# A new order of all steps for a linear-attention and squared-ReLU kernel, with stores on GpSimd and five more transposes by DMA

## The chip, the cores and the metric

The kernel runs on one core of one Trainium2 chip. A core has four compute engines that run their own instruction queues in order, and one that only issues transfers: TensorE (PE in the profile; PEld is its weight load, which overlaps the matmuls), VectorE (DVE), ScalarE (ACT), GpSimd (POOL) and SyncE (SP). Transfers between DRAM and the on-chip memory SBUF are issued by an engine's queue and carried out by 16 DMA engines. TensorE writes to PSUM, which this kernel uses as eight banks of 128 x 512 float32. The metric is the device time of the kernel in microseconds; the median of three runs before the change is 175.57 us (175.53 to 176.38).

## What is computed

```python
for t in range(S):                                       # linear attention, per batch b and head h
    cur = u * k[t] outer v[t]
    y[t] = r[t] @ (state + cur)
    state = w * state + k[t] outer v[t]                  # w decays each of the 48 rows of the state
x = y.transpose(0, 2, 1, 3).reshape(3072, 384)           # 4 x 768 tokens, 8 heads of 48
h = maximum(x @ w_in, 0)                                 # w_in 384 x 2048
out = (h * h) @ w_out                                    # w_out 2048 x 384
```

Batch 4, 8 heads, 768 steps, head size 48; all inputs and the output are float32. The kernel multiplies in bfloat16.

## The kernel before

**Tiles.** The 768 steps of a batch are cut into six chunks of 128. A unit is one chunk of one batch with all eight heads; there are 24, and unit i is chunk i // 4 of batch i % 4. Within a unit the recurrence is written as matrix products; from chunk to chunk a batch hands on a small state, S0W. The feed-forward layer then takes units in groups: units 0 and 1 by themselves (groups 0 and 1), the other 22 in pairs (groups 2 to 12).

**Steps of a unit.** Each step is a small function of the class `Do`, and its name is what the order and this text use:

- `ld.r.i`, `ld.k.i`, `ld.v.i` (L320) load 192 KB each, in rows of 192 bytes. `P0` (L342) multiplies r and k, `P1` (L346) multiplies that by u, `du` (L349) sums over the head, `dv` (L354) multiplies v by the sum.
- `kh` (L336) and `rh` (L339) scale k and r by powers of the decay and write bfloat16; for the first four units they take the powers from PSUM, later from SBUF. `vb` (L260, L262) casts v.
- The scaled r and k are transposed, either by `T` (L363, eight transposes on TensorE) and the copy `Tc` to SBUF, or by `XB` (L369), one transposing DMA of SP.
- `A` (L376), eight small matmuls; `Bm` (L384) masks the result, once for each half; `Y` (L392, L394) multiplies by v and, from the second chunk on, by the state; `xs` (L411) adds dv.
- `U` (L403) makes the state's increment; `S0` (L418), or `ts` (L421) and `S` (L424), write the new state.
- x is transposed by `X` (L429, three transposes on TensorE) and the copy `xTc`, or by `xX` (L436), one transposing DMA of SP.

**Steps of a group.** `F1.g.s` (L445) makes one PSUM bank of x @ w_in, 12 matmuls of 128 columns for a single unit, 6 of 256 for a pair; `re` (L453 on ACT, L455 on DVE) takes the maximum with zero, `sq` (L460 ACT, L462 or L464 DVE) squares. `F2.i.q` (L472) adds four matmuls of 384 columns for unit i, q = 0 to 3; `os` (L260, L262) copies the 128 x 384 result to SBUF and `out` (L489) stores it.

**Weights.** Seven of the eight pieces of w_in come as float32 by `lW.0.s` (L324, 384 KB, four buffers) and are cast by `cW.0.s`; piece 2 comes by `W.0.2` and w_out by `W.1.0` to `W.1.3` (L333), DMAs of GpSimd that cast on their way. For a pair `F1.g.s` needs piece s; for a single unit F1.g.0 needs pieces 0 and 1, F1.g.1 pieces 2 and 3, and so on. `w`, `u` and `wc` load the decay and u, `Wk`, `Wt`, `WkS`, `WtS`, `WLcol` and `WLm` make the tables from them. `Z.n.b` is n filler matmuls of no use to the result, which occupy TensorE at the start.

**What sets the order.** Nothing is planned at run time. The string ORDER lists 963 steps, each as step:engine/buffers, for example `re.1.3:D/2`: A is ACT, D is DVE, G is GpSimd, P is TensorE, S is SP, and the numbers say which buffer each new tile gets from its pool (L19; 7 buffers for each of r, k and v, 30 for hq, 2 PSUM banks each for F1 and F2). The loop at L498 issues the steps as they stand. Each engine thus has a fixed queue, and an instruction that must wait for its input or for its buffer holds back all behind it on its engine. Waits are added where one step reads what another writes.

Of the kernel before, what the change touches and what calls it, by code (L numbers as in the profile page):

```python
# [20 lines left out]
ld.r.1:S/0 w:A ld.k.1:S/0 u:S Z.48.5:P tab:A ld.k.0:S/1 ld.k.2:S/2 shw:D ld.r.0:S/1 logw:A ld.r.2:S/2 Wt:A/0 P0.1:D/0  # L21
shu:D Wk:A/1 lW.0.6:S/0 rh.1:D/0 kh.1:D ld.v.1:S/0 ld.k.3:S/3 T.1:P/0 kh.0:D/1 Z.16.5:P P1.1:G Tc.1:A/0 kh.2:D/2 rh.0:D
ld.v.3:S/1 WtS:A rh.2:D P0.2:G/1 A.1:P/1/2 WkS:A T.0:P/3 lW.0.1:S/1 Z.16.5:P P1.2:D ld.r.3:S/3 Tc.0:A/1 du.1:D/0
P0.0:D/2 cW.0.6:A ld.v.0:S/2 A.0:P/0/3 dv.1:G Bm.1.1:D/0 Z.6.5:P du.2:D/1 T.2:P/2 P1.0:G Bm.1.0:D/1 ld.v.2:S/3 Z.22.5:P
Tc.2:A/2 Bm.0.0:D/2 Bm.0.1:D/3 lW.0.0:S/2 vb.1:A/0 lW.0.5:S/3 kh.3:D/3 Y.1:P/1 cW.0.1:A lW.0.7:S/0 A.2:P/0/2 xs.1:D/0
Z.4.5:P P0.3:G/3 vb.3:A/1 du.0:D/2 lW.0.4:S/1 X.1:P/3 Z.8.5:P rh.3:D wc:S xTc.1:A/0 Bm.2.0:D/4 vb.0:A/2 T.3:P/1
ld.k.4:S/4 dv.0:D Y.0:P/3 Z.13.5:P Tc.3:A/3 vb.2:G/3 Bm.2.1:D/5 P1.3:G xs.0:D/1 A.3:P/0/2 X.0:P/1 cW.0.0:A U.0:P/3
dv.2:G Bm.3.0:D/1 Z.6.7:P xTc.0:A/1 du.3:D/3 lW.0.3:S/2 F1.1.0:P/0 Bm.3.1:D/0 ld.r.4:S/4 F1.0.0:P/1 re.1.0:D/0 W.1.0:G
W.0.2:G cW.0.7:G Y.2:P/0 Y.3:P/1 re.0.0:A/1 ld.k.5:S/5 xs.2:D/2 cW.0.5:A dv.3:D F1.1.3:P/0 cW.0.4:A X.2:P/2 F1.0.3:P/1
re.1.3:D/2 ld.r.5:S/5 xTc.2:A/0 W.1.1:G U.2:P/0 xs.3:D/3 F1.0.2:P/0 re.0.3:A/3 sq.1.3:D2/0 WLcol:A X.3:P/2 F1.1.2:P/1  # L30
re.0.2:D/4 xTc.3:A WLm:G U.3:P/1 F1.2.1:P/0 re.1.2:A/5 W.1.2:G sq.0.3:A0/1 F1.2.5:P/1 re.2.1:D/2 W.1.3:G sq.0.0:A0/2
U.1:P/2 S0.2:D re.2.5:A/3 F1.2.4:P/0 sq.0.2:D2/3 cW.0.3:A S0.0:D F1.2.7:P/1 re.2.4:D/1 sq.1.0:A0/4 F2.0.0:P/1
# [12 lines left out]
ld.k.12:S/5 sq.3.3:A0/18 Y.7:P/2 out.3:S kh.10:D/3 re.3.6:A/4 Y.6:P/1 ld.v.8:S/3 S.4:G xs.7:D/1 F1.3.2:P/0 sq.3.5:A0/19
xs.6:D/2 F1.3.7:P/1 ld.v.11:S/1 kh.8:D/0 re.3.2:A/0 kh.15:D/4 U.6:P/0 X.6:P/3 sq.3.2:A0/20 X.7:P/2 rh.8:D F2.4.0:P/1
ld.r.12:S/4 re.3.7:A/5 rh.10:D F2.5.1:P xTc.6:A/2 sq.3.4:D2/21 P1.9:D xTc.7:A U.7:P/1 T.8:P/3 vb.9:A/2 out.0:S P0.8:D/4
F1.4.0:P/0 ts.6:D/1 ld.k.11:S/0 Tc.8:A/2 P1.8:G ts.7:D/0 F1.4.4:P/1 ld.r.13:S/5 du.9:D/3 re.4.0:A/2 F2.5.2:P kh.12:G/5
re.4.4:A/3 F1.4.6:P/0 ld.r.11:S/0 sq.3.6:A0/23 sq.3.7:D2/22 vb.8:G/3 du.8:D/4 A.9:P/2/0 sq.4.4:A0/24 A.8:P/1/3 S.6:G
re.4.6:A/0 F2.5.3:P ld.v.10:S/5 Bm.8.1:D/4 F1.4.3:P/1 dv.8:G Bm.8.0:D/5 os.5:A/3 ld.k.13:S/6 F1.4.5:P/0 Bm.9.1:D/1  # L50
re.4.3:A/1 dv.9:G Y.8:P/3 Bm.9.0:D/0 re.4.5:A/5 XB.10:S/3 F2.4.1:P P0.12:G/0 xs.8:D/3 sq.4.0:A0/25 Y.9:P/1 vb.11:A/1
# [57 lines left out]
    A=["bA{0}0", "bA{0}1"],  # L109
    ld=["{0}{1}"],  # L110
    lW=["ws{0}{1}"], kh=["rk{0}"], rh=["rk{0}"], P0=["P{0}"], du=["dv{0}"], vb=["vb{0}"], T=["bT{0}"], Tc=["rkT{0}"], XB=["rkT{0}"],
    Bm=["Bm{0}{1}"], Y=["bY{0}"], xs=["xs{0}"], U=["bU{0}"], ts=["ts{0}"], X=["bX{0}"], re=["hr{0},{1}"], sq=["hq{0},{1}"],
    F1=["bH{0},{1}"], os=["os{0}"], Wk=["WkP"], Wt=["WtP"],
)


@with_exitstack
def kernel(
# [13 lines left out]
    B, H, S, D = r.shape  # L132
# [409 lines left out]
```

## Time and profile before

| quantity | value |
|---|---|
| median of the runs | 175.57 us |
| profiled execution's span, first to last instruction | 174.6 us (the median is 0.97 us longer) |
| granted TensorE clock, mean | 0.998 |
| busy: PE, DVE, ACT, POOL | 164.3, 140.6, 109.4, 69.4 us |
| filler matmuls Z within PE | 11.1 us (139 matmuls) |
| last matmul ends | 171.1 us |
| DMA: moved in all, on the queue of SP | 28.36 MB, 26.20 MB |

How it is to be read: busy time is the time in which an engine has an instruction in work. The page gives it for the whole span and in 40 slices; a table of stretches gives it for any window. An engine that is busy without a break for a long stretch sets the pace there. The table of groups gives the mean duration of each kind of instruction and the idle time ahead of it with what ended it. A timeline lists single instructions with their start, duration and, in brackets, the idle time before them. For a DMA the engine's row shows the issue only; the landing is seen in the page's table of DMA issues (median us from issue to landing) or in an instruction that waited for it.

### The profile page before, as it was taken

To read this page: it belongs to the slowest core of one execution; us is meant where nothing else is said; L and a number is where in the kernel's file an instruction comes from. 1 tells how busy PE (TensorE), PEld (TensorE's weight loads), DVE (VectorE), ACT (ScalarE), POOL (GpSimd) and SP (SyncE) were. 2 spreads that over 40 slices of the span, in tenths; PEclk is the share of its full clock that TensorE was granted. 3 is DMA by queue.
4 is the path that set the end of the run, shared out by engine and by line. 5 is a ranking of instruction groups with operands and counts; after the bars stand their busy time and mean duration, and the time that the engine had idled before them with its cause. 6 is when DMAs were issued, how large, how long until landed. Compare 5 with 4: busy or idle time off the path is not lost.

```text
span 174.6 us, 4605 instructions
## 1 busy us (share of the span) xinstructions
PE 164.3 (94%) x1813; PEld 127.1 (73%) x1813; DVE 140.6 (80%) x279; ACT 109.4 (63%) x203; POOL 69.4 (40%) x85
## 2 busy tenths in 40 slices
PE   3978599999999999999999999999999999999991
PEld 3967488866778777877767787777778677787760
DVE  5779677799899989999989898899988667853620
ACT  3578479549499987786677669669478142164410
POOL 5253834044366594925373960700950302000000
PEclk9999999999999999999999999999999999999999
DMA  4989999989799999999998989989931422110041
GB/s 99 228 194 240 320 200 237 207 155 213 144 205 177 231 217 165 233 157 252 152 214 187 195 164 220 160 196 230 164 94 26 158 90 71 24 45 4 0 165 61
DMA packets 102421, 28.36 MB, mean 162 GB/s; under 512 B 94840, under 2 KB 102400, under 8 KB 102400
## 3 DMA queue, kind: packets, MB, share of 16 engines
q1 hardware_dynamic: 100504, 26.20, 72.6%
q0 software_dynamic: 1744, 1.77, 6.3%
q8 instruction: 14, 0.23, 0.5%
q10 hardware_dynamic: 152, 0.10, 0.2%
q14 instruction: 7, 0.06, 0.1%
HBM read 20.46 MB, written 4.72 MB: 144 GB/s over the span
## 4 chain that ended last, share of the span: by engine, by line
PE 84%; DMA 6%; SPq 4%; POOL 1%; issue 1%; ACT 0%; DVE 0%; POOLq 0%
PE bank L472 36%; PE bank L445 36%; DMA wsa<-in_moe_w_in_dram 6%; SPq L320 4%; PE bank L376 3%; PE bank L394 2%; PE bank L392 2%; PE bank L403 2%; PE bank L363 2%; PE bank L429 1%; POOL W L262 1%; SPq L324 0%; POOL urow L218 0%; ACT vb L260 0%; DVE os L262 0%
## 5 line engine op out<-in xcount | busy, mean ns | idle before, releaser
L445 PE MATMUL bank<-xT,W 128*128 128x256 bf16 (+1 forms) x624 | 74.4, 264 | 2.3 <-ACT W L260 2.1
L472 PE MATMUL bank<-W,hq 128*128 128x384 bf16 x384 | 73.6, 326 | 0.0
L453 ACT ACTIVATE hr<-bank 128x512 bf16<-128x512 f32 x71 | 42.0, 597 | 36.8 <-PE bank L445 34.2
L445 PEld LDWEIGHTS <-W 128*128 128x128 bf16 x624 | 55.4, 98 | 12.6 <-ACT W L260 2.2
L472 PEld LDWEIGHTS <-hq 128*128 128x128 bf16 x384 | 35.6, 98 | 17.8
L460 ACT ACTIVATE hq<-hr 128x512 bf16<-128x512 bf16 x57 | 34.7, 629 | 2.5 <-DVE hr L455 2.2
L384 DVE TENSOR_TENSOR Bm<-bank,maskJT 128x512 bf16<-128x512 f32 x48 | 31.4, 682 | 3.1 <-PE bank L376 3.0
L346 POOL TENSOR_TENSOR P<-P,ub 128x384 f32<-128x384 f32 x14 | 15.2, 1087 | 30.2 <-DVE P L342 27.4
L354 POOL TENSOR_TENSOR dv<-ldv,du 128x384 f32<-128x384 f32 x19 | 16.4, 874 | 25.0 <-DVE du L349 21.0
L455 DVE TENSOR_SCALAR hr<-bank 128x512 bf16<-128x512 f32 x25 | 17.1, 688 | 11.2 <-PE bank L445 7.5
L464 DVE TENSOR_TENSOR hq<-hr 128x512 bf16<-128x512 bf16 x35 | 15.0, 456 | 1.7 <-ACT hr L453 1.7
L411 DVE TENSOR_TENSOR xs<-bank,dv 128x384 bf16<-128x384 f32 x24 | 13.2, 553 | 3.2 <-PE bank L394 2.5
L481 PE MATMUL bank<-identity 128*128 128x128 bf16 x139 | 11.1, 244 | 2.7 <-POOL identity masks.py:199 2.7
L260 ACT COPY os<-bank 128x384 f32<-128x384 f32 (+1 forms) x18 | 8.4, 469 | 8.1 <-PE bank L472 8.1
L342 POOL TENSOR_TENSOR P<-ldr,ldk 128x384 f32<-128x384 f32 x11 | 11.3, 1025 | 4.8 <-DMA ldr<-in_r_dram 4.8
L349 DVE TENSOR_REDUCE du<-P 128x8 f32<-128x384 f32 x24 | 12.9, 542 | 0.0
L260 ACT COPY rkT<-bank 128x1024 bf16<-128x1024 bf16 x10 | 10.1, 1016 | 3.4 <-PE bank L363 3.3
L481 PEld LDWEIGHTS <-identity 128*128 128x128 bf16 x139 | 9.8, 112 | 2.9 <-POOL identity masks.py:199 2.7
L424 POOL TENSOR_TENSOR S0W<-ts,WLm 128x384 bf16<-128x384 f32 x7 | 7.4, 1061 | 10.0 <-PE bank L472 6.7
L394 PE MATMUL bank<-vb,Bm 128*128 128x48 bf16 x192 | 10.8, 183 | 0.5 <-ACT vb L260 0.5
L394 PEld LDWEIGHTS <-Bm 128*128 128x128 bf16 x192 | 9.5, 96 | 1.5 <-issue 0.8
L260 ACT COPY xT<-bank 128x384 bf16<-128x384 bf16 x14 | 6.5, 478 | 5.1 <-PE bank L429 5.1
(62 smaller groups left out, 167.1 us busy)
## 6 DMA issues: line engine op xcount, KB each, us to landing
ldr<-in_r_dram SPq DMA_DIRECT2D x24, 192.0 KB, 3.8
ldk<-in_k_dram SPq DMA_DIRECT2D x24, 192.0 KB, 3.9
ldv<-in_v_dram SPq DMA_DIRECT2D x24, 192.0 KB, 3.6
out_dram<-os SPq DMA_DIRECT2D x23, 192.0 KB, 2.1
wsa<-in_moe_w_in_dram SPq DMA_DIRECT2D x7, 384.0 KB, 5.9
W<-in_moe_w_out_dram POOLq DMA_DIRECT2D x4, 384.0 KB, 7.6
rkT<-rk SPq DMA_TRANSPOSE x14, 4.2
W<-in_moe_w_in_dram POOLq DMA_DIRECT2D x1, 192.0 KB, 8.8
```

The costliest lines, as they stand in the source:

```text
L260: e.copy(o, a)
L346: e.tensor_mul(t, t, ub)
L354: e.tensor_mul(dvb[slot[f"dv{i}"]], loaded("v", i), t)
L384: e.tensor_mul(Bmb[slot[f"Bm{i}{h}"]], heads(bank(f"bA{i}{h}"), 128), mask_b)
L394: e.matmul(y[:, hc, D * h : D * (h + 1)], m[h][:, hc, :], vb[:, 2 * hc + h, :], start=(c == 0), stop=True, skip_group_check=True,)
L445: e.matmul(hp[:, fi, :], W1[f // 2][:, c, 128 * (f % 2) : 128 * (f % 2 + 1)], xt[:, c, :], start=(c == 0), stop=(c == CCH - 1), skip_group ...
L453: e.activation(hr, hp, AF.Relu)
L455: e.tensor_scalar_max(hr, hp, 0.0)
L460: e.activation(hq, hr, AF.Square)
L464: e.tensor_mul(hq, hr, hr)
L472: e.matmul(bank(f"bO{i}", "bO")[:, 0:d_model], hqb[slot[f"hq{g},{f // m}"]][:, at : at + L], W2[q][:, f % 4, :], start=(f == 0), stop=(f = ...
L481: e.matmul(banks[b][:, 0:128], identity, identity, start=True, stop=True, skip_group_check=True)
```

## The change

All steps are put in a new order, and many change their engine or buffer; 956 are left. The F2 steps go from 96 to 92, and two steps of a new kind, F2c, are added. Pools, buffers and the functions of the other steps are the same.

- Loads stay on SP in another order: the first eight are k.2, r.0, u, r.2, r.1, k.0, v.0, r.3, and the two small DMAs of `wc`, which stood behind the weight loads, now come tenth.
- Fifteen of the 24 stores of SP are issued by GpSimd instead; nine stay on SP, and half of the last tile on ACT, where it was.
- Units 7, 8 and 11 are transposed by `XB` instead of `T` and `Tc` (7 T, 17 XB), units 13 and 19 by `xX` instead of `X` and `xTc` (12 X, 12 xX).
- Element-wise work moves between engines, mostly to GpSimd:

| step | before | after |
|---|---|---|
| P0 | 13 DVE, 11 POOL | 7 DVE, 17 POOL |
| P1 | 10 DVE, 14 POOL | 8 DVE, 16 POOL |
| kh | 19 DVE, 5 POOL | 9 DVE, 15 POOL |
| rh | 18 DVE, 6 POOL | 13 DVE, 11 POOL |
| vb | 19 ACT, 2 DVE, 3 POOL | 7 ACT, 6 DVE, 11 POOL |
| S | 9 DVE, 7 POOL | 3 DVE, 13 POOL |
| cW | 6 ACT, 1 POOL | 3 ACT, 4 POOL |
| sq | 57 ACT, 39 DVE | 36 ACT, 60 DVE |
| re | 71 ACT, 25 DVE | 77 ACT, 19 DVE |
| os | 18 ACT, 7 DVE | 16 ACT, 9 DVE |

- The last unit's F2 is made in two column runs, each over all 16 row blocks and in a PSUM bank of its own: columns 256 to 383 first, then 0 to 255. The halves of the last store are cut there too, instead of at 192.

GpSimd's queue from its first step to the last of the weight loads, before and after:

```
before: P1.1 P0.2 dv.1 P1.0 P0.3 vb.2 P1.3 dv.2 W.1.0 W.0.2 cW.0.7 W.1.1 WLm W.1.2 W.1.3
after:  P0.2 P0.0 P1.2 P1.0 P0.1 P1.1 dv.0 WLm P0.3 vb.1 rh.4 P1.3 cW.0.7 dv.2 vb.3 kh.4 cW.0.0 W.0.2
        P0.4 cW.0.4 kh.5 W.1.0 W.1.1 cW.0.3 W.1.2 P0.5 vb.4 dv.4 W.1.3
```

SP's queue over the same time:

```
before: r.1 k.1 u k.0 k.2 r.0 r.2 lW.0.6 v.1 k.3 v.3 lW.0.1 r.3 v.0 v.2 lW.0.0 lW.0.5 lW.0.7 lW.0.4 wc
        k.4 lW.0.3 r.4 k.5 r.5 k.7
after:  k.2 r.0 u r.2 r.1 k.0 v.0 r.3 k.1 wc k.3 v.2 lW.0.6 v.1 r.4 lW.0.7 lW.0.1 lW.0.0 v.3 k.4 lW.0.5
        lW.0.4 k.5 lW.0.3 r.5 v.4 v.5 r.6 k.9 r.7 k.7
```

The diff, with the lists cut to a few of their lines:

```diff
 ORDER = """
-ld.r.1:S/0 w:A ld.k.1:S/0 u:S Z.48.5:P tab:A ld.k.0:S/1 ld.k.2:S/2 shw:D ld.r.0:S/1 logw:A ld.r.2:S/2 Wt:A/0 P0.1:D/0
...
-W.0.2:G cW.0.7:G Y.2:P/0 Y.3:P/1 re.0.0:A/1 ld.k.5:S/5 xs.2:D/2 cW.0.5:A dv.3:D F1.1.3:P/0 cW.0.4:A X.2:P/2 F1.0.3:P/1
...
-F2.20.3:P sq.12.5:A0/0 F2.23.1:P os.20:D/2 F2.23.2:P out.20:S F2.23.3:P out.19:S F2.22.0:P/1 out.21:S os.23:D/1
-F2.22.1:P out.23:S F2.22.2:P F2.22.3:P os.22.0:A/2 os.22.1:D out.22.0:A out.22.1:S
+ld.k.2:S/0 tab:A w:A shw:D Z.16.4:P ld.r.0:S/0 u:S Z.22.5:P shu:D ld.r.2:S/1 logw:A P0.2:G/0 ld.r.1:S/2 Wk:A/0 kh.2:D/0
...
+cW.0.7:G dv.2:G vb.3:G/3 X.1:P/2 U.1:P/0 Bm.3.0:D/4 Y.2:P/1 xTc.1:A/1 kh.4:G du.3:D/3 Z.4.4:P F1.1.3:P/1 lW.0.5:S/0
+lW.0.4:S/2 S0.1:D S0.0:D cW.0.0:G F1.0.3:P/0 ld.k.5:S/5 W.0.2:G re.0.3:A/0 xs.2:D/2 lW.0.3:S/1 dv.3:D ld.r.5:S/5 Y.3:P/2
...
+os.20:A/2 sq.12.6:D2/10 F2.23.3:P F2c.22.1:P/1 os.23:D/1 F2c.22.0:P/0 os.22.1:D/0 out.23:S os.22.0:A out.20:G out.22.0:A
+out.22.1:S out.21:S
 """
...
-    F1=["bH{0},{1}"], os=["os{0}"], Wk=["WkP"], Wt=["WtP"],
+    F1=["bH{0},{1}"], F2c=["bO{0}{1}"], os=["os{0}"], Wk=["WkP"], Wt=["WtP"],
...
+        def F2c(e, i, h):
+            g, j = group_of[i]
+            n = len(GROUP[g])
+            m = 4 // n
+            c = part(h)
+            for f in range(FCH):
+                at = L * n * (f % m) + L * j
+                e.matmul(
+                    bank(f"bO{i}{h}", "bO")[:, c],
+                    hqb[slot[f"hq{g},{f // m}"]][:, at : at + L],
+                    W2[f // 4][:, f % 4, c],
+                    start=(f == 0), stop=(f == FCH - 1), skip_group_check=True,
+                )
+
...
         def os(e, i, half=None):
             c = part(half)
-            copy(e, osb[slot[f"os{i}"]][:, c], bank(f"bO{i}", "bO")[:, c])
+            o = f"bO{i}" if half is None else f"bO{i}{half}"
+            copy(e, osb[slot[f"os{i}"]][:, c], bank(o, "bO")[:, c])
...
     def part(half):
-        return slice(0, d_model) if half is None else slice(d_model // 2 * half, d_model // 2 * (half + 1))
+        return slice(0, d_model) if half is None else (slice(0, 256), slice(256, d_model))[half]
```

## The prediction

> **What bounds the kernel now.** I read the page's slices first, then the chain of waits, then a table of three stretches, then the timelines of ACT, GpSimd and SP over the first 30 us. The page and the table of stretches (columns: length, then busy us of PE, PEld, DVE, ACT, POOL):
>
> ```profile
> PE   3978599999999999999999999999999999999991
> ...
> POOL 5253834044366594925373960700950302000000
> ...
> PE 84%; DMA 6%; SPq 4%; POOL 1%; issue 1%; ACT 0%; DVE 0%; POOLq 0%
> ```
>
> ```profile
> 0.00:24.15 24.15, 17.41 (x275) 15.48 (x276) 17.82 (x45) 13.57 (x20) 12.00 (x24) 1.00 0.92 213
> 24.15:171.09 146.94, 146.91 (x1538) 111.58 (x1538) 122.41 (x234) 95.49 (x183) 57.38 (x62) 1.00 0.79 157
> 171.09:174.60 3.51, 0.00 (x0) 0.00 (x0) 0.36 (x1) 0.32 (x1) 0.00 (x0) 0.89 0.17 56
> ```
>
> From 24.15 us to 171.09 us TensorE has work in 146.91 of 146.94 us: nothing waits there that counts. PE is busy for 164.3 us in all, of which 11.1 us are the filler matmuls Z, so 153.2 us are useful. The last matmul ends at 171.09, so 171.1 - 153.2 = 17.9 us are lost ahead of the dense stretch, and 3.5 us lie behind it. The kernel is thus three numbers: start 17.9, useful TensorE work 153.2, tail 3.5. What makes the start, from the timelines of POOL and ACT and the page's DMA issues:
>
> ```profile
> 17.38 0.58 POOL L262 CAST vb<-ldv 128x384 bf16<-128x384 f32 x1 [0.45 <-DMA ldv<-in_v_dram]
> ...
> 20.54 0.76 POOL L333 DMA_DIRECT2D W<-in_moe_w_in_dram  x1
> 23.23 0.87 POOL L262 CAST W<-wsa 128x768 bf16<-128x768 f32 x1 [1.93 <-DMA wsa<-in_moe_w_in_dram]
> ```
>
> ```profile
> 20.70 0.86 ACT L260 CAST W<-wsa 128x768 bf16<-128x768 f32 x1 [2.61 <-DMA wsa<-in_moe_w_in_dram]
> ```
>
> ```profile
> W<-in_moe_w_out_dram POOLq DMA_DIRECT2D x4, 384.0 KB, 7.6
> ...
> W<-in_moe_w_in_dram POOLq DMA_DIRECT2D x1, 192.0 KB, 8.8
> ```
>
> Loads from SP land in the order of issue, and the casts that wait for them date them: the twelfth r/k/v load with two weight loads before it at 17.4, the third weight load at 20.7, two more at 23.2 (1.25 us each). W.0.2, one eighth of w_in, is loaded by GpSimd: issued at 20.54, landed 8.8 us later at 29.3. Its first user, F1.0.1, stands behind 12.8 us of useful matmuls, so at 17.9 + 12.8 = 30.7: no wait.
>
> **The change, part by part.**
>
> *TensorE work.* Three T go (8 transposes, 0.45 us each in the chain of waits) and two X (3 transposes, 0.17 us): 3 x 0.45 + 2 x 0.17 = 1.7 us, all in the dense stretch, so all on the path. The last F2 as 16 matmuls of 128 columns and 16 of 256: 128 columns stream in 0.67 / 12 = 0.056 us (F1 of the groups of one), 256 in 0.109, so 16 x 0.165 = 2.6 us, as four F2 of 0.65 before: 0. Useful work after: 151.5. The bound from above is the weight loads, 32 instead of 16 at 98 ns; the F1 of the single groups pay 56 ns a matmul with a weight load each, so nothing is taken.
>
> *The five DMA transposes* cost SP 1.2 to 1.5 us each to issue and land in 2.9 (xX) or 4.2 us (XB). SP gives up 15 stores of 0.4 to 1 us and the 25 us of waits ahead of stores that its waits list, so it has room. The shortest xX lead is Y.20 to F1.11.3, 4.6 us of PE work; xs 0.55 plus 2.9 plus a DVE instruction waited for, 0.7, is 4.2. Taken 0, bound +1 (3.7 us is the slowest landing, on the few short leads).
>
> *The start.* Counted in instructions by their rows. Before F1.1.3, the first F1, SP now has 12 r/k/v loads, three weight loads and the two small wc loads, about what it had ahead of the 20.7 landing. lW.0.1 is that third weight load: 20.7. Behind it lW.0.0 (1.25) 22.0, ld.v.3 23.0 and ld.k.4 24.0 (1024 packets of 15.6 ns over 16 engines, 1.0 us each), lW.0.5 and lW.0.4 25.3 and 26.5. ACT: cW.0.1 waits to 20.7, then 0.87 + xTc.0 0.48 + vb.2 0.51 + xTc.1 0.48: F1.1.3 at 23.1 (before: F1.1.0 at 21.6).
> GpSimd now carries four cW, eleven vb, and P0, P1, kh, rh of the first units. From its list: vb.3 waits for ld.v.3 at 23.0, kh.4 for ld.k.4 (24.0 to 25.0), cW.0.0 25.0 to 25.9, so W.0.2, which waits for nothing, is queued behind two landings and issued at 25.9 where it was 20.5. It lands 8.8 later: 34.7. Behind it P0.4 and cW.0.4 to 28.6, kh.5 and W.1.0 to W.1.1 after that. F1.2.4 needs cW.0.4: useful work ahead of it 9.0, so 28.6 - 9.0 = 19.6 lost. F1.0.1 needs W.0.2: 12.7 ahead, 34.7 - 12.7 = 22.0 lost. Later users (F2.0.0 with 16.8 ahead, W.1.0 issued near 29.6 and 7.6 on its way: 37.2, 20.4) ask less. So the start goes from 17.9 to 22.0: **+4.1**. Lower end: GpSimd waiting for nothing, from its first landing at 6.1 through 15.8 us of instructions, issues W.0.2 at 21.9 and all is in time: 0. Upper end: 1 us more per late landing, as W of both kinds spread from 7.0 to 8.8 us: +6. I take 4.1, as the row is that of the same transfer in the same crowd of loads (DMA share 0.92 over the start).
>
> *The middle.* GpSimd grows from 69 us to 112 by rows: P0 11 to 17, kh 5 to 15, rh 6 to 11, S 7 to 13, at about 1.0 each; vb 3 to 11 at 0.6; 15 stores at 0.77 (the row of W). ACT loses 23 us, DVE 8. Summed along the queues by the rows without waits (GpSimd from 6.3, DVE from 4.5, TensorE from 17.9), GpSimd's producers stand 7 us ahead of their TensorE users near 40 us and 13 or more after 70; DVE's 5 us near 60 and 9 after 90, where before it stood 3.3 ahead and caused no idle TensorE. GpSimd enters that stretch some 5 us late by the landings above, TensorE 4. I take 0, and bound it by the next point.
> Row first: DVE instructions with both inputs in SBUF and GpSimd's never run together (timelines of POOL and of DVE).
>
> ```profile
> 59.90 0.99 POOL L336 TENSOR_TENSOR rk<-ldk,Wkhat 128x384 bf16<-128x384 f32 x1
> ...
> 69.18 1.25 POOL L346 TENSOR_TENSOR P<-P,ub 128x384 f32<-128x384 f32 x1 [2.23 <-DVE P L342]
> 70.39 1.31 POOL L339 TENSOR_TENSOR rk<-ldr,Wt 128x384 bf16<-128x384 f32 x1
> ```
>
> ```profile
> 60.17 1.00 DVE L464 TENSOR_TENSOR hq<-hr 128x512 bf16<-128x512 bf16 x1
> ...
> 69.49 1.35 DVE L336 TENSOR_TENSOR rk<-ldk,Wkhat 128x384 bf16<-128x384 f32 x1
> ```
>
> hq takes 1.00 instead of 0.42 and ends 0.28 after GpSimd's rk; the DVE rk takes 1.35 instead of 0.55 and ends 0.41 after GpSimd's P; GpSimd's next ends 0.86 after that. So a GpSimd product holds DVE off for about 0.86 us, a DVE one GpSimd for 0.41 (hq 0.28). By these, both together hold the inputs 89 us before and 113 after: under the 125 us in which they stand, so no bound by itself. All DVE delays before add up to 5 us of 18 that chance meetings would give (101 instructions, GpSimd holding 0.42 of the time, 0.43 us on average).
> The Trainium skill, SBUF — State Buffer, "Who interferes with whom", says the second of the two blocks until the first has finished; by that the price would be the whole 1.0 us rather than 0.86, 16% more delay, and the sum the same.
>
> *The tail.* Before, ACT copies half of the last tile (0.32), DVE the other half after it (171.44, 0.36), and SP issues the last store at 171.8. After, the 128 columns end 1.7 us before the 256 (16 x 0.109), their copy and store lie beside these, and only ACT's copy of 256 columns (about 0.37, between 0.32 for 192 and 0.48 for 384) stands behind the last matmul: -0.35. out.21 and out.23 go ahead on SP beside the last matmuls. Bounds -0.7 (DVE's copy and an issue) to +0.7 (SP's three issues in a row late).
>
> Sum against the profiled execution's 174.6: -1.7 + 4.1 - 0.35 = +2.05, so 176.65. The median of the runs is 175.57, 0.97 more than this span; **177.6 us**.
>
> **The rivals.**
> 1. *The start is no later* (faster). GpSimd's waits vanish if v.3 and k.4 land 2 us earlier, or W.0.2 comes in 7.0 us, the fastest of the W; it decides at a landing of 30.5, where F1.0.1 would stand. Then 174.6 - 1.7 - 0.35 + 0.97 = 173.5. For it: the same transfer was early before, and the other queues nearly allow it (DVE's sum puts re.0.2, and F1.1.1 behind it, at 32.5: 18.8 lost). Against: sixteen r/k/v and weight loads stand ahead of v.3. 0.22.
> 2. *Half of it*: W.0.2 lands in 7.6 after an issue at 24: 31.6, then cW.0.4 sets the start at 19.6: +1.7 - 2.05 + 175.57 = 175.2. 0.13.
> 3. *Shared inputs.* The order was laid out for one timing; with the start late, DVE and GpSimd meet by chance. GpSimd then holds 0.62 of the time: 100 DVE instructions x 0.62 x 0.43 = 27 us of delay, against 9 to 13 us of room in DVE's queue plus 8 less work: past some 13 us TensorE waits, +5 to +9 in the end, 183 to 187. For it: twice the GpSimd work. Against: before, 5 us of 18. 0.14.
> 4. *Stores on GpSimd starved.* If each issue waits for the DVE instruction that runs, 15 x 0.55 = 8 us more on GpSimd, with 13 in hand: +0 to +2 on the forecast, 179. Against: the W issues took 0.70 to 0.89 us with DVE at work. 0.04. The Trainium skill, SBUF — State Buffer, "SBUF: two separate sides", states this trap for a GpSimd-issued DMA beside DVE copies between SBUF tiles (620 ns grow to about 3100 ns); by its figures the 15 stores would cost an estimated 37 us, and no run here shows it.
>
> **How the numbers follow.** The forecast (start late, middle dense) has 0.47, by itself 176.6 to 179.5 (start +3.1 to +6). Slower: forecast and rivals 3 and 4, less what falls short of 0.5%: 0.64; faster 0.22; same 0.14. 0.5% (0.9 us) is about what a measurement of this kernel tells from no change. The range leaves the lower half of rival 1 and the upper of rival 3 outside: 173.6 to 183.
>
> **What would show it.** Right: in the timeline of POOL two waits on loads of v and k between 18 and 25 us and the W of w_in issued near 26; an idle stretch of PE ahead of L445 at 32 to 35 released by that DMA; T x7, X x12; PE dense after 36; the last store 0.35 sooner after the last matmul. Wrong: the W of w_in issued by 22 (rival 1), or PE idle after 40 with DVE or POOL as the releaser (rival 3), shown by DVE L464 and L336 means well over 0.5 us.

## The result and the profile after

The changed kernel takes 211.13 us (median of 4 runs, 208.53 to 212.21), the kernel before 175.97 us beside it (4 runs, 175.53 to 176.73). The ratio is 1.192, 95% interval 1.183 to 1.201: slower by 35 us, where 2 us were forecast. The ratio and its interval leave out the slowest execution, 212.21 us, 1.8% above the fastest; the profile is of that one. It has a span of 210.3 us, and its last matmul ends at 206.81.

The page of the changed kernel: the 40 slices (5.26 us each) of PE, DVE and the granted clock, the chain of waits, and three groups.

```profile
PE   4957876998964999398997899949905999999993
...
DVE  5668889979999897989999999995999686726540
...
PEclk9996999999997999969999999988995899999998
...
DVE 42%; PE 39%; issue 6%; DMA 6%; SPq 4%; POOL 1%; ACT 1%; DVEq 0%; POOLq 0%
...
L472 PE MATMUL bank<-W,hq 128*128 128x384 bf16 x368 | 72.5, 334 | 6.6 <-DVE hq L464 6.0
...
L464 DVE TENSOR_TENSOR hq<-hr 128x512 bf16<-128x512 bf16 x56 | 49.2, 897 | 3.0 <-ACT hr L453 2.8
...
L504 POOL DMA_DIRECT2D out_dram<-os x15 | 8.5, 570 | 37.7 <-ACT os L260 19.4
```

The dense row of nines of PE is gone. It breaks at 63 us, 84, 137 and 152 us (the digits 4, 3, 4 and 0), and VectorE is busy for 90% or more there. In the chain PE falls from 84% to 39% and DVE comes up from 0 to 42%. One square, hq, costs 897 ns on average; before it was 456:

```profile
L464 DVE TENSOR_TENSOR hq<-hr 128x512 bf16<-128x512 bf16 x35 | 15.0, 456 | 1.7 <-ACT hr L453 1.7
```

The stores on GpSimd themselves are cheap, 570 ns each.

The table of stretches (length; then busy us and instructions of PE, PEld, DVE, ACT, POOL; clock, DMA share, GB/s), and behind it the first stretch of the kernel before:

```profile
24.15:66.00 41.85, 33.29 (x397) 26.11 (x394) 39.19 (x57) 20.33 (x35) 30.75 (x34) 0.99 1.00 187
66.00:206.81 140.81, 122.78 (x1158) 89.90 (x1158) 117.41 (x177) 59.65 (x112) 66.59 (x76) 0.94 0.54 115
```

```profile
24.15:66.00 41.85, 41.85 (x496) 33.11 (x497) 37.50 (x72) 32.92 (x62) 21.28 (x26) 1.00 1.08 199
```

TensorE stands idle for 8.6 us of the first stretch and 18.0 of the second. VectorE is busy in 39.19 of 41.85 us of the first one with 57 instructions, 0.69 us each; before it did 72 there in 37.50. Where the idle time of TensorE went, from its list of waits (total us, times, longest):

```profile
PE bank L376 <- DVE xs L411: 7.3, 1, 7.3
PE bank L472 <- DVE hq L464: 6.0, 2, 3.3
PE bank L429 <- DVE xs L411: 5.9, 2, 4.8
```

Four of these five waits are over 2 us, and each ends with a VectorE instruction that itself took several microseconds or was queued behind one that did. The longest, from the timelines of POOL, DVE and PE (start, duration):

```profile
148.05 0.54 POOL L504 DMA_DIRECT2D out_dram<-os  x1 [8.73 <-ACT os L260]
148.61 0.84 POOL L354 TENSOR_TENSOR dv<-ldv,du 128x384 f32<-128x384 f32 x1
149.40 1.01 POOL L346 TENSOR_TENSOR P<-P,ub 128x384 f32<-128x384 f32 x1
...
154.95 1.93 POOL L424 TENSOR_TENSOR S0W<-ts,WLm 128x384 bf16<-128x384 f32 x2
156.84 0.69 POOL L262 CAST vb<-ldv 128x384 bf16<-128x384 f32 x1
```

```profile
149.96 7.21 DVE L464 TENSOR_TENSOR hq<-hr 128x512 bf16<-128x512 bf16 x1
157.09 1.80 DVE L336 TENSOR_TENSOR rk<-ldk,Wkhat 128x384 bf16<-128x384 f32 x1
...
159.29 0.55 DVE L411 TENSOR_TENSOR xs<-bank,dv 128x384 bf16<-128x384 f32 x1
```

```profile
159.89 0.58 PE L376 MATMUL bank<-rkT 48*128 48x128 bf16 x7 [7.33 <-DVE xs L411]
```

GpSimd issues a store at 148.05 and 0.02 us behind it goes on with nine products without a gap, to 156.88. The square that begins at 149.96 and by itself takes 0.41 us ends at 157.17, 0.3 us behind the end of the last product. In the kernel before every VectorE instruction got in after one product. Six other long ones look alike: a store issued by GpSimd, a run of two to five instructions without a gap, most of them products, and one VectorE instruction that lasts until the run ends or breaks (dv at 60.95 took 4.52 us, hq at 84.27 took 4.03, at 135.46 3.62).

The waits cost TensorE more than their own length. In four stretches, which begin during such a wait or within 1.2 us after it (3.41 us each at 65.51, 89.40 and 140.60, and 6.83 at 157.67), the granted clock is 0.50, and the same 12 matmuls of F1 take 2.74 us there and 1.47 behind it:

```profile
157.67:164.50 6.83, 4.61 (x27) 3.04 (x27) 6.83 (x13) 1.42 (x3) 0.81 (x1) 0.50 0.41 84
```

```profile
160.40 2.74 PE L445 MATMUL bank<-xT,W 128*128 128x256 bf16 x12
...
165.99 1.47 PE L445 MATMUL bank<-xT,W 128*128 128x256 bf16 x12
```

TensorE has work in 14.2 of these 17.1 us, so some 7 us are lost to the clock (an estimate: half of the 14.2). In the kernel before the clock is whole until its last matmul has ended. What sets it was not tested.

From here on "excess" is the time by which VectorE's products and casts with all inputs in SBUF exceed their undisturbed durations (0.55 us, 0.41 for a bfloat16 square, 0.38 for a cast). Before it was 4.9 us in 11 instructions, none over 1 us. After it is 45.9 us in 44, of which 28.4 us are in ten instructions of over 1 us each, called long waits here. Those ten are the new thing. Seven of them, with 24.6 us, stand behind a store as above; two at the start, 1.5 and 1.0 us, stand beside the issues of weight loads, and one, 1.25 us, comes right behind the longest.

### The profile page after: what moved, and what is told of

Read it like the earlier page. It is cut to its first block, busy times and chain, and to the rows that moved or that the text cites. A ratio compares the mean times of both kernels' runs of the same rounds, so it can differ in the third digit from the quotient of the medians.

```text
span 210.3 us, 4582 instructions
## 1 busy us (share of the span) xinstructions
PE 173.6 (83%) x1799; PEld 131.8 (63%) x1799; DVE 172.8 (82%) x272; ACT 92.1 (44%) x166; POOL 113.8 (54%) x139
## 4 chain that ended last, share of the span: by engine, by line
DVE 42%; PE 39%; issue 6%; DMA 6%; SPq 4%; POOL 1%; ACT 1%; DVEq 0%; POOLq 0%
PE bank L472 17%; PE bank L445 16%; DVE hq L464 12%; DVE Bm L384 6%; DVE dv L354 4%; DVE rk L339 3%; DMA wsa<-in_moe_w_in_dram 3%; DVE xs L411 3%; DVE P L346 2%; DVE ts L421 2%; DVE rk L336 2%; DVE du L349 2%; DVE P L342 2%; SPq L320 2%; DMA ldk<-in_k_dram 2%
## 5 line engine op out<-in xcount | busy, mean ns | idle before, releaser
L472 PEld LDWEIGHTS <-hq 128*128 128x128 bf16 x368 | 35.5, 100 | 25.9 <-DVE hq L464 6.8
L464 DVE TENSOR_TENSOR hq<-hr 128x512 bf16<-128x512 bf16 x56 | 49.2, 897 | 3.0 <-ACT hr L453 2.8
L504 POOL DMA_DIRECT2D out_dram<-os x15 | 8.5, 570 | 37.7 <-ACT os L260 19.4
L424 POOL TENSOR_TENSOR S0W<-ts,WLm 128x384 bf16<-128x384 f32 x13 | 14.1, 1084 | 21.7 <-DVE ts L421 21.7
L460 ACT ACTIVATE hq<-hr 128x512 bf16<-128x512 bf16 x36 | 22.3, 628 | 0.1
L342 POOL TENSOR_TENSOR P<-ldr,ldk 128x384 f32<-128x384 f32 x17 | 17.2, 1017 | 4.0 <-DMA ldr<-in_r_dram 2.9
L455 DVE TENSOR_SCALAR hr<-bank 128x512 bf16<-128x512 f32 x19 | 12.8, 683 | 7.2 <-PE bank L445 4.0
L376 PE MATMUL bank<-rkT 48*128 48x128 bf16 x192 | 8.7, 221 | 11.1 <-DVE xs L411 7.3
L339 POOL TENSOR_TENSOR rk<-ldr,Wt 128x384 bf16<-128x384 f32 x11 | 11.9, 1086 | 8.5 <-DMA ldr<-in_r_dram 8.5
L336 POOL TENSOR_TENSOR rk<-ldk,Wkhat 128x384 bf16<-128x384 f32 x15 | 16.2, 1082 | 0.4 <-DMA ldk<-in_k_dram 0.4
L376 PEld LDWEIGHTS <-rkT 48*128 48x128 bf16 x192 | 5.6, 95 | 14.8 <-issue 10.7
L260 ACT COPY os<-bank 128x384 f32<-128x384 f32 (+1 forms) x16 | 7.5, 471 | 16.5 <-PE bank L472 11.6
L495 PE MATMUL bank<-identity 128*128 128x128 bf16 x139 | 11.8, 262 | 2.7 <-POOL identity masks.py:199 2.7
```

The source lines that it names most:

```text
L336: e.tensor_mul(rk[slot[f"rk{i}"]][:, 1, :, 0:D], loaded("k", i), early("WkP") if i < EARLY else Wkhat)
L339: e.tensor_mul(rk[slot[f"rk{i}"]][:, 0, :, 0:D], loaded("r", i), early("WtP") if i < EARLY else Wt2)
L342: e.tensor_mul(P0b[slot[f"P{i}"]], loaded("r", i), loaded("k", i))
L460: e.activation(hq, hr, AF.Square)
L464: e.tensor_mul(hq, hr, hr)
L472: e.matmul(bank(f"bO{i}", "bO")[:, 0:d_model], hqb[slot[f"hq{g},{f // m}"]][:, at : at + L], W2[q][:, f % 4, :], start=(f == 0), stop=(f = ...
```

## The experiments

The first four ask which part of the change brings it, the next ask for the mechanism by itself, the last for the remaining terms. Times are of one execution unless an interval is given. The kernel before took 175.1 to 175.4 us beside e1 to e6, e8 and m1 to m5, on two chips. On a third it took 176.8 beside e10, and 176.16 to 181.19 with a median of 178.85 beside e7, e9, c2 and c3.

### e1: the stores back on SyncE

```diff
-... out.2:G ... out.0:G ... out.3:G ... out.6:G ...
+... out.2:S ... out.0:S ... out.3:S ... out.6:S ...      (all 15)
```

> The changed kernel with its fifteen GpSimd stores issued by SP again, in the same places of the order. Theory A (a run of GpSimd products keeps DVE's instructions with two SBUF inputs waiting, for the whole run and not for one product): the products are all still there, so DVE's excess stays above 30 us and the time above 195 us. Theory B (the stores on GpSimd are the cause: three of the eight longest DVE waits begin while a store is being issued there): the long waits go, DVE's hq mean falls from 0.90 us to below 0.55, the time to 180 us or less.

Measured: 191.84 us. The excess falls to 31.3 us in 54 instructions, and that in waits of over 1 us from 28.4 us to 1.5. So the long waits come with the stores on GpSimd, and cost some 19 us. But 16.7 us over the kernel before remain, and 31 us of excess in single meetings: the time lies between what the two theories said.

### e2: the engines as before, the order and the GpSimd stores as after

```diff
-... P0.0:G ... P1.2:G ... dv.0:G ... rh.4:G ... cW.0.0:G ... kh.4:G ... sq.1.2:A0 ...
+... P0.0:D ... P1.2:D ... dv.0:D ... rh.4:D ... cW.0.0:A ... kh.4:D ... sq.1.2:D2 ...
```

(P0, P1, kh, rh, S, vb, dv, cW, re, sq, os and the copies, each on the engine that the kernel before gives it.)

> The changed kernel's order, with P0, P1, kh, rh, S, vb, dv, cW, re, sq, os and the copies on the engines that they had before; stores stay on GpSimd. Theory A: GpSimd is back at some 65 us of products, DVE's excess falls from 46 us to below 12, time 176 to 184 us. Theory B: the stores are still there, so above 195 us. Theory C (the order itself makes TensorE wait, whatever the engines): above 195 us with DVE's hq near 0.45 us.

Measured: 193.55 us, excess 15.1 us in 27, 2.9 of it in one wait of over 1 us. With fewer products on GpSimd all but one of the long waits go as well, though the stores are still there: it takes both. The time met none of the three expectations; theory A had 176 to 184 us for it.

### e3: VectorE's squares on ScalarE

```diff
-... sq.0.3:D2/0 ... sq.1.0:D2/1 ... sq.0.0:D2/2 ...
+... sq.0.3:A0/0 ... sq.1.0:A0/1 ... sq.0.0:A0/2 ...      (all 56)
```

> The changed kernel with the 56 squares of DVE that read hr twice from SBUF moved to ACT (0.63 us each there, ACT's sum 137 us). Theory A: 27 us of the 41 us of extra DVE delay sat in these; with them off DVE the time falls to 180 to 192 us, and what is left of the delay sits in dv, rh, kh, P and S of DVE. Theory B: the stores on GpSimd are left, so above 200 us.

Measured: 195.62 us, excess 27.2 us in 27, of which 13.7 in four long waits. The time lies between the two expectations, 180 to 192 and above 200. Taking away the victims that were hit most helps by 15 us, but the long waits then fall on VectorE's other products; TensorE's largest wait is again 6.6 us for an xs. The squares are where it shows, not what brings it.

### e4: the kernel before with the same 15 stores on GpSimd

```diff
-... out.2:S ... out.0:S ... out.3:S ...
+... out.2:G ... out.0:G ... out.3:G ...      (the 15 of the change)
```

> The kernel before with the same fifteen stores issued by GpSimd, nothing else changed. Theory A: GpSimd had room, so 175 to 178 us. Theory B: 185 us or more, with DVE waits of several us that begin during a store's issue.

Measured: 175.19 us beside 175.11: nothing. In its timeline of GpSimd at most two products stand directly behind a store, then GpSimd waits or issues again:

```profile
87.63 0.58 POOL L489 DMA_DIRECT2D out_dram<-os  x1
88.24 1.01 POOL L342 TENSOR_TENSOR P<-ldr,ldk 128x384 f32<-128x384 f32 x1
89.19 1.01 POOL L339 TENSOR_TENSOR rk<-ldr,Wt 128x384 bf16<-128x384 f32 x1
90.13 0.58 POOL L489 DMA_DIRECT2D out_dram<-os  x1
93.53 1.00 POOL L346 TENSOR_TENSOR P<-P,ub 128x384 f32<-128x384 f32 x1 [2.82 <-DVE P L342]
```

The store alone is harmless. What differs in the changed kernel is the longer run of products behind it.

### e5: the order alone

Stores on SyncE (the edit of e1) and the engines as before (the edit of e2).

> The changed kernel's order of steps, with the 15 GpSimd stores back on SyncE and the element-wise steps on the engines that the kernel before gave them; only the order, the DMA transposes and the last F2 stay changed. If the loss is the sum of two things, the stores on GpSimd and the meetings of GpSimd products with VectorE instructions that read SBUF twice: VectorE's excess falls under 12 us, no instruction waits over 1 us beyond its own time, and the time is 178 to 183 (the two single undoings gave 191.8 and 193.6, so some 19 and 17 us each of 36). If the order itself is bad (late loads, queues out of step): over 188 with little excess on VectorE. If the forecast had been right but for the meetings: 176 to 179.

Measured: 190.94 us, excess 13.1 us in 27, none over 1 us. A miss: the two undoings do not add up, and the time is in the range that was given for a bad order. e1 and e5 differ by 0.9 us, e2 and e5 by 2.6, and the changed kernel lies 17 to 20 us above any of the three. Putting the old engines into an order that was laid out for others makes queues late in its own way (TensorE's waits are spread over ts, Bm, xs, vb and hr there), so e2 and e5 do not price the order by itself; e6 below, the same order with the new engines, does that better. What exactly bounds e5 was not followed further.

### m1, m2 and m3: runs of products added to the kernel before

Three runs of six GpSimd products, each run waiting for one hq of groups 10, 11 and 12, where GpSimd had little to do. Nothing reads what they write. m1 has the runs alone, m2 a GpSimd DMA directly ahead of each, m3 that DMA and then a later hq to wait for.

```diff
+        def R(e, n, g, s):
+            a = hqb[slot[f"hq{g},{s}"]][:, 0 : H * D].rearrange("p (h d) -> p h d", h=H)
+            for k in range(n):
+                e.tensor_mul(scr, Wt2 if k else a, ub)
+        def N(e, g, s):
+            e.dma_start(out=scd, in_=hqb[slot[f"hq{g},{s}"]][:, 0 : H * D])
-... sq.10.3:D2/15 sq.10.5:D2/17 ...
+... sq.10.3:D2/15 N.10.3:G R.6.10.3:G sq.10.5:D2/17 ...      (m2; m1 without N)
```

> The kernel before with 18 products added on GpSimd, in three runs of six (each writes a tile that nothing reads); each run first waits for one hq and no DMA issue of GpSimd stands before it. GpSimd had little to do there, VectorE squares hq. If a VectorE instruction always gets in after one GpSimd product: longest square up to 1.4 us, 1 to 3 us of excess more, time +0 to +2 us. If an unbroken run of GpSimd products by itself holds VectorE off: squares of 3 to 6 us, one or two for each run, time +3 to +8 us.

> The same three runs of six products, each directly behind a DMA that GpSimd issues (a copy of that hq from SBUF to SBUF, nothing reads it). If a run that begins right behind a DMA issue holds VectorE off until the run ends: squares of 3 to 6 us at each of the three runs, time +3 to +8 us over the kernel before, and 3 us or more over the runs without the issue. If the issue plays no part: the same as those within 1 us, longest square as there.

> The same DMAs and the same runs of six products, but each run first waits for a later hq, so that GpSimd stands idle between the issue and the run. If only a run without a gap behind the issue holds VectorE off: like the runs without issues, longest square up to 1.4 us, time +0 to +2 us. If an issue changes GpSimd's way for all that follows, gap or not: squares of 3 to 6 us here too.

Measured: 181.33, 180.85 and 177.94 us; excess 12.3, 11.5 and 9.5 us, no long wait but two of 1.1 us excess in m2. In m1 VectorE did get in after each product, but the time rose by 6 us and not by 0 to 2: with squares queued one behind another each of them waits for a product. m2 was a miss for the idea that an issue ahead is enough. m3 lies 2.8 us above the kernel before, where 0 to 2 were expected. But all six products wrote one tile in these three, so that each waited for the one ahead, and between them GpSimd stood still for some 0.07 us (in m2 from 147.62 + 0.93 to 148.62). That gap was not in the changed kernel's run.

### m4 and m5: the same with products that need not wait for each other

```diff
-    scr = const.tile([128, H, D], FP32, name="scr")
+    scr = [const.tile([128, H, D], BF16, name=f"scr{n}") for n in range(6)]
-                e.tensor_mul(scr, Wt2 if k else a, ub)
+                e.tensor_mul(scr[k], Wt2 if k else a, ub)
```

m4 is m1 with this edit, m5 is m2 with it. The products now write bfloat16 as well, in both.

> The kernel before with the three runs of six added products, each product now writing a tile of its own in bfloat16, so that none has to wait for the one ahead (in the run with one tile 0.07 to 0.12 us lay between some). No store or other issue ahead. If alternation holds for any run that follows no issue: every square gets in after one product, longest up to 1.4 us, and the time is that of the run with one tile, 180 to 182. If it was the small gap that let VectorE in: squares of 3 to 6 us, time 181 to 186.

> The same with a DMA issue on GpSimd directly ahead of each run. If an issue followed by products without a gap holds VectorE off to the run's end: squares of 3 to 6 us in at least two of three runs, and 2 us or more of time above the same without the issue. If the issue plays no part: as the same without the issue, within 1 us.

Measured: m4 180.40 us, m5 195.92. Three DMA issues of 0.6 us make 15.5 us. The first run in m4, GpSimd and VectorE:

```profile
145.64 1.04 POOL L484 TENSOR_TENSOR scr<-hq,ub 128x384 bf16<-128x384 bf16 x1 [1.41 <-DVE hq L466]
146.64 5.53 POOL L484 TENSOR_TENSOR scr<-Wt,ub 128x384 bf16<-128x384 f32 x5
```

```profile
145.15 2.94 DVE L466 TENSOR_TENSOR hq<-hr 128x512 bf16<-128x512 bf16 x4
```

and in m5:

```profile
145.93 0.61 POOL L488 DMA_DIRECT2D scd<-hq  x1 [1.63 <-DVE hq L467]
146.56 0.93 POOL L485 TENSOR_TENSOR scr<-hq,ub 128x384 bf16<-128x384 bf16 x1
147.43 4.78 POOL L485 TENSOR_TENSOR scr<-Wt,ub 128x384 bf16<-128x384 f32 x5
```

```profile
145.22 7.28 DVE L467 TENSOR_TENSOR hq<-hr 128x512 bf16<-128x512 bf16 x4
```

```profile
PE bank L475 <- DVE hq L467: 13.5, 3, 5.7
```

In m4 five products take 5.53 us, as VectorE's squares come between them, and four squares take 2.94. In m5 the five products run undisturbed in 4.78 us and the four squares take 7.28: one of them alone 6.28 us, through all six products (3.96 and 6.25 in the other two runs). TensorE waits 13.5 us for these three. With each of the waits its clock is 0.50 again, for 17.1 us in all with work in 12.7 of them: some 6 of the 15.5 us (an estimate, as above). This is the mechanism of the changed kernel, brought into the other one by three issues.

### e8, e10 and e9: copies behind each store of the changed kernel

e8 puts one one-input copy of 144 columns behind each GpSimd store, e10 two copies of 16 columns to two tiles, e9 the same two copies to one tile, so that the second waits for the first.

```diff
             e.dma_start(out=out_v[(i % B) * NCH + i // B][:, c], in_=osb[slot[f"os{i}"]][:, c])
+            if e is nc.gpsimd:                       # e9
+                e.tensor_copy(scr, ub[:, 0, 0:16])
+                e.tensor_copy(scr, ub[:, 1, 0:16])
```

> The changed kernel, with one one-input copy of 128x144 (about 0.4 us, read by nothing) on GpSimd directly behind each of its 15 stores. If VectorE is held off by products that follow a store without a gap: the waits of over 1 us go (28.4 us in 10 waits before, under 5 us in at most 3 now), and the time falls to that with the stores on SyncE, 190 to 196, in spite of 6 us more work on GpSimd. If it is the issue itself, or GpSimd's load, that costs: 207 to 216, with the long waits still there.

> The changed kernel with the same two copies of 16 columns behind each GpSimd store, now to two tiles, so that the second need not wait for the first and GpSimd runs from the store into its products without a gap. If the gap is what counts: long waits back, over 20 us in VectorE instructions of more than 1 us excess, and 205 to 214. If any two instructions behind the store are enough: 188 to 195 and at most 5 us in such waits.

> The changed kernel with two tiny copies (16 columns each, to one tile, so that the second waits for the first) on GpSimd directly behind each of its 15 stores; no products left out. If a short gap on GpSimd behind the issue is what gives VectorE its turn back: the waits over 1 us go (at most 3, under 5 us) and the time falls to 190 to 197. If the gap has to come between the products themselves, as it did in the run with one scratch tile: 205 to 214 with the long waits, as with the one copy (208.5).

Measured: e8 208.48 us, e10 204.86, e9 190.21; excess in waits of over 1 us 28.6, 20.4 and 1.2 us. e10 and e9 differ in one thing: in e9 the second copy waits for the first, and GpSimd stands still for 0.06 us between them. The same store and run as above, in e9, GpSimd and VectorE:

```profile
133.48 0.54 POOL L505 DMA_DIRECT2D out_dram<-os  x1 [3.38 <-ACT os L261]
134.01 0.21 POOL L507 CAST scr<-ub 128x16 bf16<-128x16 f32 x1
134.29 0.20 POOL L508 CAST scr<-ub 128x16 bf16<-128x16 f32 x1
134.45 0.82 POOL L355 TENSOR_TENSOR dv<-ldv,du 128x384 f32<-128x384 f32 x1
...
137.16 1.30 POOL L343 TENSOR_TENSOR P<-ldr,ldk 128x384 f32<-128x384 f32 x1
138.42 1.31 POOL L337 TENSOR_TENSOR rk<-ldk,Wkhat 128x384 bf16<-128x384 f32 x1
```

```profile
135.78 0.73 DVE L465 TENSOR_TENSOR hq<-hr 128x512 bf16<-128x512 bf16 x1
136.43 1.18 DVE L337 TENSOR_TENSOR rk<-ldk,Wkhat 128x384 bf16<-128x384 f32 x1
137.53 1.35 DVE L340 TENSOR_TENSOR rk<-ldr,Wt 128x384 bf16<-128x384 f32 x1
```

and in e10:

```profile
141.50 0.20 POOL L508 CAST scr<-ub 128x16 bf16<-128x16 f32 x1
141.66 0.83 POOL L355 TENSOR_TENSOR dv<-ldv,du 128x384 f32<-128x384 f32 x1
```

```profile
143.00 7.21 DVE L465 TENSOR_TENSOR hq<-hr 128x512 bf16<-128x512 bf16 x1
```

In e9 the first copy ends at 134.22 and the second starts at 134.29; from there on the engines take turns, and the square takes 0.73 us. In e10 each instruction starts before the end of the last, and the square takes 7.21 us as in the changed kernel. So this gap behind the issue ends the holding off for all the run that follows, and an instruction without a gap does not. Whether it is the standing still or the wait that brings it, these runs do not tell apart. e9 lies 14.7 us below e10, on the same chip, and 18 to 22 below the changed kernel: adding 30 useless instructions undoes half of the 35 us or more.

### e6 and e7: GpSimd without products of two inputs

Each GpSimd product is left out and replaced by two one-input copies, of 384 columns of the first input and 144 (96 for S) of the second, so every wait stays. e6 has its stores on SyncE, e7 on GpSimd.

```diff
+    def product(e, o, a, b):
+        if e is not nc.gpsimd:
+            e.tensor_mul(o, a, b)
+            return
+        e.tensor_copy(o, a)
+        ...
+            e.tensor_copy(t, b[:, 0:3, :])
-            e.tensor_mul(P0b[slot[f"P{i}"]], loaded("r", i), loaded("k", i))
+            product(e, P0b[slot[f"P{i}"]], loaded("r", i), loaded("k", i))
```

> The changed kernel with its stores on SyncE, and every GpSimd product of two SBUF inputs (P0, P1, kh, rh, dv, S: 90 of them) replaced by two one-input copies of about the same time together (384 columns of the first input to the output, 128 columns of the second to a scratch tile, about 0.58 + 0.39 us), so that every wait stays and the products are left out. If the stores-on-SyncE version's 191.8 comes from shared inputs: VectorE's excess falls from 31 us to under 4, and the time to 178 or less. If it is the order itself: excess falls as well, but the time stays above 188.

> The changed kernel as it is, 15 stores on GpSimd, with every GpSimd product replaced by two one-input copies (the products are left out) as in the version with its stores on SyncE, which took 180.1. If the stores cost only through products that follow them: no VectorE wait over 1 us, and 179 to 183 (15 issues of 0.57 us more on GpSimd). If the issues hold VectorE off by themselves or delay GpSimd: over 186.

Measured: e6 180.09 us, excess 9.0 us; e7 180.81 us, excess 11.6 us, 1.4 of it in one wait, beside the issues of two weight loads. e7's time is as expected: without products of two inputs 15 stores on GpSimd cost next to nothing. e6 came nearest to the first of its expectations, but missed both numbers, 4 us of excess and 178 us. From e1 to e6 11.7 us go, from e9 to e7, beside each other, 9.4 us. Part of that may be GpSimd's load, as the copies are a little shorter than the products (busy 93.8 us in e6, 111.2 in e1). What is left over the kernel before, 2 to 5 us, is the price of the rest of the change, close to the forecast. The largest waits of TensorE that are left in e6, the first of them before 17 us, where the kernel before waits 0.4:

```profile
PE bank L391 <- ACT rkT L275: 3.3, 3, 1.1
...
PE bank L460 <- DMA xT<-xs: 1.7, 1, 1.7
PE bank L378 <- DVE rk L213: 1.6, 1, 1.6
```

### c2 and c3: DMA transposes in the kernel before

```diff
-... T.8:P/3 ... Tc.8:A/2 ...
+... rh.8:D XB.8:S/2 ...          (c2: 7, 8 and 11; c3: 8 and 11)
-... X.19:P/2 ... xTc.19:A ...
+... xs.19:D/4 xX.19:S ...        (c2: 10 and 19; c3: 19)
```

> The kernel before with three T (units 7, 8, 11) and two X (units 10, 19) made by DMA transposes of SyncE, each issued directly behind the step that writes its input; nothing else moves. If the term of the forecast holds, 1.7 us of TensorE work gone from a dense stretch and nothing for the DMAs: 1.4 to 1.8 us faster. If the DMA transposes land late for units 7 and 10, which have 4.4 to 4.5 us of TensorE work between input and use: within 0.7 us of the kernel before, or slower, with PE idle ahead of A or F1 released by a DMA.

> The same with T of units 8 and 11 and X of unit 19 only, which have 4.9, 7.2 and 6.3 us between input and use: 2 x 0.45 + 0.17 = 1.07 us less TensorE work. If the term holds: 0.8 to 1.1 us faster. If SyncE's queue is late with them: no faster.

Measured against the kernel before: c2 1.024 (95% interval 1.018 to 1.029), c3 1.0045 (1.0002 to 1.0089), which is the same. TensorE's work did shrink, but it now waits; in c2 and in c3:

```profile
PE bank L445 <- DMA xT<-xs: 2.4, 1, 2.4
PE bank L376 <- DMA rkT<-rk: 1.7, 1, 1.7
```

```profile
PE bank L445 <- DMA xT<-xs: 1.5, 1, 1.5
```

In c2 it waits for two of the added transposes, those of units 10 and 8, and not for that of unit 7, which was expected to be late; with the longer wait the clock is 0.50 for 3.41 us. In c3 it waits 1.54 us at 109.88 for a transpose that was there before: SyncE's queue has become late for others. SyncE keeps its 15 stores in c2 and c3, so they do not test the room that the forecast saw in its queue without them; e7, where the stores are on GpSimd, still has 2.7 us of waits on DMA transposes. Neither version beats the kernel before, and nothing else here does.

## Why the prediction was wrong

The step that failed is the middle: "I take 0, and bound it by the next point", and the next point's price for a meeting, one GpSimd product. Step by step:

- **Useful TensorE work, -1.7.** The counts came (T 56 matmuls, X 36), and the last F2 in two column runs took 2.80 us in its row, of which 0.16 is the end of its last matmul, so 2.64 against 2.6: right. "The five DMA transposes... Taken 0, bound +1" holds no longer as a rule: in the kernel before five of them cost 4.1 us of waits and c2 is slower by 2.6 us. The 3.7 us of that bound is the slowest landing of an xX; the slowest XB before took 5.0. In the changed kernel the waits on such transposes can't be seen beside the larger ones, and e6 has 2.3 us of waits on DMA transposes. The 151.5 us of useful work is what e7 shows, 152.4; the changed kernel has 161.8 (173.6 less 11.8 for Z), and most of the difference is the clock of 0.50. The forecast had no term for that.
- **The start, +4.1.** Size near, cause wrong, so the size is luck. By the same counting 23.1 us are lost at 35.15 us (forecast 22.0). The GpSimd queue did what was said: vb waits for ld.v.3, kh for ld.k.4, and the load of w_in behind them is issued at 24.75 (forecast 25.9). But it landed in 6.0 us, not 8.8, at 30.7, and F1.0.1 did not wait for it. The idle stretch of 1.77 us is there, released by VectorE's rh of unit 5, which ended at 34.86 in a queue that had hardly a gap from 21.5 us on (the same wait, 1.6 us, is in e6, where GpSimd has no products). The clock was also 0.50 from 17.72 to 21.13 us, as it was not before:

```profile
34.31 0.55 DVE L339 TENSOR_TENSOR rk<-ldr,Wt 128x384 bf16<-128x384 f32 x1
```

```profile
34.91 0.40 PE L363 MATMUL bank<-identity,rk 128*128 128x128 bf16 x4 [1.77 <-DVE rk L339]
```

- **The tail, -0.35.** 3.44 us from the last matmul to the end, against 3.58 counted in the same way: -0.14. ACT's copy took the 0.37 that was estimated; the larger last store took the rest.
- **Engine loads.** GpSimd's 112 us came (113.8), in part because two errors cancel: the list leaves out two P1 and three cW, 4.8 us by their rows, and the 15 stores took 0.57 us each and not 0.77, 3 us less. VectorE's 8 us less came too, but cannot be seen: it is busy for 172.8 us, 32 more than before, while its excess grew by 41, so its own work fell by 9.
- **Rival 3, shared inputs, 0.14, 183 to 187.** The right place and the right sign in the profile (L464 and L336 at 0.90 and 1.00 us), but mis-sized twice. Its 27 us of delay by single meetings are what e1 shows (31.3), and they cost 9 to 12 us, not 5 to 9. That the kernel before had 5 of 18 was counted against it; that was a property of the order before. And on top of single meetings came the long waits, ten with 28.4 us of excess, seven of them through runs behind a store, and some 20 us of time, which its price per meeting, 0.43 us, left no room for.
- **Rival 4, stores on GpSimd starved, 0.04, +0 to +2.** The stores matter, but the other way round: the issues took 0.57 us each, undisturbed, and it was VectorE that starved behind them. The Trainium skill, SBUF — State Buffer, "SBUF: two separate sides", warns of VectorE holding up a GpSimd DMA; no run here shows that, and in m5 it is VectorE that waits behind the DMA.
- **One product per meeting.** The forecast weighed the rule that the second of the two blocks until the first has finished, and found 16% more delay. The Trainium skill, SBUF — State Buffer, "Who interferes with whom", calls the pair of ports that VectorE and GpSimd share an exclusive lock, held for the whole instruction by whoever issues first. The traces agree in the kernel before, in m1, m4 and e9, where turns are taken at the end of an instruction. They disagree in m5, e10 and the changed kernel, where a square waits through up to eight of GpSimd's products.

In spans of the profiled executions the way from 174.6 to 210.3 us is: order, start and transposes 4.5 (e7, 179.1), meetings one by one together with GpSimd's added work 9.4 (e9, 188.5), holding off behind stores 21.8. Measured to the execution of 208.53 us, with a span of 206.6, the last part is 18.1. About 6 us of it are not waits but TensorE's clock (useful matmuls busy for 161.8 us, in e9 155.3). These runs are from several chips, whose kernel before differs by up to 3.7 us, so each number has that uncertainty; on its own chip e7 is 2.0 us above the kernel before. The forecast had the first of the three.

What stays open: why an issue followed without a gap takes away VectorE's turn. No view shows what goes on inside GpSimd. Whether the holding off also needs some minimum number of products, how long a wait must be to bring the clock down, and whether an order with fewer GpSimd products behind its issues could use the change's other parts, was not tried.

## What to carry to other kernels

An instruction's price beside another engine is not a constant of the pair: read from the timeline not only how long a meeting lasted, but what let the waiting engine in, and ask whether the new order still has it. Before a DMA is moved to an engine that also computes, look at what stands directly behind it in that engine's queue; here a store in front of idle time was free, and a store in front of two to nine products cost microseconds on another engine. And a kernel that runs dense has an order in which short leads are just met: work taken off its bounding engine by DMAs comes back as waits unless the leads are longer than the landing.

## What the runs showed of the hardware

- A GpSimd DMA issue followed without a gap by GpSimd products of two SBUF inputs holds off a VectorE instruction with both inputs in SBUF until the run ends or breaks: 7.21 us for a 0.41 us square in the changed kernel, 6.28, 3.96 and 6.25 us in m5. The 0.02 us between the issue and the first product do not count as a gap here. The same run without the issue, m4, has no wait of more than one product; its longest square takes 1.22 us.
- A gap of about 0.06 us on GpSimd behind the issue (e9) restores the turns; one or two copies without a gap (e8, e10) do not. In the changed kernel a gap of 0.08 us in the middle of a run let a square in (it began at 112.33 and took 3.08 us, with GpSimd idle from 115.10 to 115.19); a one-input cast without a gap, at 136.38 in another run, did not.
- While VectorE is held off GpSimd runs at 0.95 us a product; when they take turns a product takes 1.17 to 1.31 us.
- With one-input copies on GpSimd in place of products VectorE's mean excess per meeting was 0.2 us (9.0 us in 45, e6), with products 0.6 (31.3 in 54, e1).
- With TensorE's long waits the granted clock was 0.50 for 3.41 or 6.83 us: in the changed kernel at 65.51, 89.40, 140.60 and 157.67, in m5 at 149.69, 166.75 and 183.82. These waits thus cost more than their own length. What length of wait brings it on the traces do not fix.
